# Sliding-window attention feeding a gated MLP on one core: attention tiles of 96 queries replaced by blocks of 32 queries by 64 keys

## The chip, the cores and the metric

The kernel runs on 1 core of one Trainium2 chip. The metric is the device time of one execution in microseconds (us). The kernel before took 1094.05 us (median of 3 runs, 1093.78 to 1095.33). About 0.2% of that, some 2.2 us, is what a measurement can tell from no change.

The engines by the profile's names: PE multiplies matrices (PEld is its loading of the stationary operand, which overlaps), DVE is the vector engine, ACT the scalar engine, POOL the third elementwise engine, SP issues most transfers.

## What is computed

```python
q, k, v: (8, 8, 576, 64)          # batch, heads, positions, head size, float32
rel = pos[:, None] - pos[None, :]
plain   = (rel >= 0) & (rel < 32)                     # heads 0 to 3
dilated = (rel >= 0) & (rel < 128) & (rel % 4 == 0)   # heads 4 to 7
attn = softmax(where(mask, q @ k.T / 8, -1e9)) @ v
x = attn as (4608 tokens, 512)    # 8 heads side by side
g, val = x @ w_gate, x @ w_val    # 512 -> 1536
out = (silu(g) * val) @ w_out     # 1536 -> 512
```

Every query sees at most 32 keys: the 32 last positions, or every fourth of the last 128.

## The kernel before, in words

The 4608 tokens are cut into 12 chunks of 384 (CH). The MLP of a chunk takes 12 steps (NF), one for each 128 of the 1536 hidden features; `s` counts all 144 steps, `ci, f = divmod(s, 12)`. A step issues 36 products of 128x128 by 128x384 in float32r: 12 for the gate into `bank_g` and 12 for the value into `bank_v` (`gv_mm`, L457), and, for the step before, 12 into four output banks (`out_mm`, L493). The factor three comes from a split: x, h and the weights are kept as a high part rounded to float32r and a low part, and high-high, high-low and low-high are added up. Around the products stand `act_tanh` (ACT, L465), `dve_u` and `dve_h` (DVE, L470 and L474), `h_hi` (ACT, L478) and `h_lo` (POOL, L483). `dve_u` empties `bank_g`, so the next step's gate products wait for it.

The weights are loaded during the first chunk, as 24 units of raw 64-bit words, two for each step: a transfer by SP (`w_load`, L198), E on ACT (L207), B on DVE (two operations, L213 and L214), H on ACT (L224) and L on POOL (L228). B of a unit also issues the load of a later unit. The last four units share one buffer, `spare["r"]`.

The attention of chunk c fills `x_hi[c % 2]` and `x_lo[c % 2]` for the chunk's MLP. A chunk has four packs, one for each pair of heads (`ORDER`: the two dilated pairs, then the two plain ones). It is done in three ways:

- Chunk 0, ahead of the MLP, already in blocks of 32 queries by 64 keys (`b_scores` to `b_x_lo`, L532 to L603), from an order written out by hand (L648). A block product has 64 contracting rows and 32 output columns, so that two heads use PE's two halves of rows and four blocks its four quarters of columns. Each float32 product is two instructions in the trace. Twelve blocks make three groups of 128 rows.
- Chunk 1, during chunk 0's MLP, in tiles of 96 queries (64 in the dilated packs that cross a sequence's end), two tiles of a pair of heads at a time: mask and scores into `bank_s` (`scores_pair`, L295 and L298), maximum (L313), four exponentials with sums (L322), division on POOL (L350).
- Chunks 2 to 11, one tile at a time: `split_hi` and `split_lo` (L358 on ACT, L363 and L364 on POOL) cut queries and keys into float32r parts, `scores` multiplies twice with 256 columns (L370), `maxima` adds parts and mask and takes the maximum on DVE (L383 to L385), `exps` runs two exponentials with sums on ACT (L392), `norm` divides on POOL (L400).

In the last two, `transposes` (L408) turns two tiles for both heads (four instructions), `pt_copy` (L413) takes the result to SBUF, and once for a pack `av_mm` (L421) multiplies with v, one head in each half of PE's columns, two instructions a product; `x_copy_hi` (L440) and `x_copy_lo` (L444) write x. Chunk 1 has 18 tiles, chunks 2 to 11 have 166, in 40 packs of 4 or 5.

The order of the work is the program's order, which the scheduler of the language keeps except where data is not there yet. The loops from L690 spread a chunk's tiles over 10 to 12 steps of the chunk before: scores behind the gate products (after `act_tanh`, ahead of `dve_u`) or behind `h_lo`, transposes behind the value products, `av_mm` after `out_mm`.

## Time and profile before

| what | value |
|---|---|
| time, median of 3 runs | 1094.05 us |
| the profiled execution's own time | 1093.62 us |
| its span on the core | 1091.8 us |
| first product of the MLP starts | 30.66 us |
| first product of step 12 (chunk 1) starts | 142.44 us |
| first product of step 132 (chunk 11) starts | 1007.85 us |
| PE busy from 142.44 us on | without a gap, in all but the last microseconds |
| transfers, mean over the span | 78 GB/s |

In a row of a group: line, engine, operation, output <- inputs, size of the stationary operand (rows*columns), size of the moving one (partitions x elements), count, then total busy us, mean ns of one, idle us before them and what ended it. A row of the chain or of a timeline begins with its start and its length in us. Mean ns of a PE instruction is its latency; instructions overlap, so what one costs is the distance between starts.

### The profile page before, as it was taken

To read this page: it belongs to the slowest core of one execution; us is meant where nothing else is said; L and a number is where in the kernel's file an instruction comes from. 1 tells how busy PE (TensorE), PEld (TensorE's weight loads), DVE (VectorE), ACT (ScalarE), POOL (GpSimd) and SP (SyncE) were. 2 spreads that over 40 slices of the span, in tenths; PEclk is the share of its full clock that TensorE was granted. 3 is DMA by queue.
4 is the path that set the end of the run, shared out by engine and by line. 5 is a ranking of instruction groups with operands and counts; after the bars stand their busy time and mean duration, and the time that the engine had idled before them with its cause. 6 is when DMAs were issued, how large, how long until landed. Compare 5 with 4: busy or idle time off the path is not lost.

```text
span 1091.8 us, 19600 instructions
## 1 busy us (share of the span) xinstructions
PE 1058.4 (97%) x7106; PEld 1027.4 (94%) x7106; DVE 509.5 (47%) x1309; ACT 489.5 (45%) x1416; POOL 517.2 (47%) x681
## 2 busy tenths in 40 slices
PE   6887999999999999999999999999999999999997
PEld 4776999999999999999999999999999999999997
DVE  5797445445444444345444454444444444442211
ACT  4565544454445445445444544444444544542111
POOL 1564555555455555454545554454555555541111
PEclk7888999999999999999999999999999999999999
DMA  7763332232122213112213222113122221300000
GB/s 284 246 213 110 125 99 62 62 90 71 47 86 69 69 46 99 53 53 81 66 55 90 61 63 81 52 54 91 53 55 79 75 66 49 98 19 2 29 1 30
DMA packets 62801, 85.48 MB, mean 78 GB/s; under 512 B 5008, under 2 KB 58608, under 8 KB 62704
## 3 DMA queue, kind: packets, MB, share of 16 engines
q1 hardware_dynamic: 62416, 83.64, 25.5%
q8 instruction: 56, 0.92, 0.4%
q10 hardware_dynamic: 288, 0.59, 0.1%
q14 instruction: 41, 0.34, 0.1%
HBM read 74.77 MB, written 9.44 MB: 77 GB/s over the span
## 4 chain that ended last, share of the span: by engine, by line
PE 90%; DVE 5%; ACT 2%; DMA 2%; issue 1%; POOLq 0%; POOL 0%; ACTq 0%; SPq 0%; DVEq 0%
PE bg L457 27%; PE bo L493 26%; PE bv L457 26%; PE bs L370 4%; PE bt L421 3%; PE bt L408 3%; DVE y L214 2%; DVE y L213 1%; DMA words<-w 1%; ACT words L207 1%; DMA qkb<-qkb 1%; ACT e L322 1%; ACT w L224 0%; DVE ma L313 0%; PE fx L561 0%
## 5 line engine op out<-in xcount | busy, mean ns | idle before, releaser
L457 PE MATMUL bg<-xh,w 128*128 128x384 f32 x1152 | 326.1, 344 | 3.4 <-DVE xl L603 3.4
L457 PE MATMUL bv<-xh,w 128*128 128x384 f32 x1152 | 319.8, 338 | 0.0
L493 PE MATMUL bo<-hh,w 128*128 128x384 f32 x1152 | 300.6, 342 | 0.0
L457 PEld LDWEIGHTS bg<-xh,w 128*128 128x128 f32 x1152 | 213.5, 190 | 9.4 <-DVE xl L603 3.8
L483 POOL TENSOR_TENSOR hl<-t,hh 128x384 fp32r<-128x384 f32 x144 | 146.8, 1020 | 152.8 <-PE bo L493 144.3
L363 POOL TENSOR_TENSOR cmb<-raw,cmb 128x256 fp32r<-128x256 f32 x166 | 122.4, 738 | 197.1 <-ACT cmb L358 186.4
L457 PEld LDWEIGHTS bv<-xh,w 128*128 128x128 f32 x1152 | 211.2, 188 | 0.6
L465 ACT ACTIVATE t<-bg 128x384 f32<-128x384 f32 x144 | 70.8, 491 | 308.1 <-PE bg L457 278.3
L493 PEld LDWEIGHTS bo<-hh,w 128*128 128x128 f32 x1152 | 203.1, 188 | 1.0 <-issue 1.0
L493 PE MATMUL bo<-hl,w 128*128 128x384 f32 x576 | 194.5, 338 | 1.5 <-POOL hl L483 1.5
L457 PE MATMUL bg<-xl,w 128*128 128x384 f32 x576 | 195.7, 340 | 0.0
L457 PE MATMUL bv<-xl,w 128*128 128x384 f32 x576 | 194.4, 338 | 0.0
L392 ACT ACTIVATE s<-s,nm 96x128 f32<-96x128 f32 x332 | 130.8, 395 | 113.5 <-DVE nm L385 111.9
L383 DVE SCALAR_TENSOR_TENSOR s<-bs,consts 96x256 f32<-96x256 f32 x166 | 69.6, 419 | 239.7 <-PE bs L370 238.2
L400 POOL TENSOR_TENSOR s<-s,zr 96x256 f32<-96x256 f32 x166 | 101.6, 612 | 134.2 <-DVE zr L399 110.1
L470 DVE SCALAR_TENSOR_TENSOR t<-t,bg 128x384 f32<-128x384 f32 x144 | 78.5, 545 | 84.7 <-ACT t L465 84.5
L493 PEld LDWEIGHTS bo<-hl,w 128*128 128x128 f32 x576 | 108.1, 188 | 2.2 <-POOL hl L483 2.2
L474 DVE SCALAR_TENSOR_TENSOR t<-t,bv 128x384 f32<-128x384 f32 x144 | 79.7, 553 | 64.9 <-PE bv L457 63.9
L457 PEld LDWEIGHTS bg<-xl,w 128*128 128x128 f32 x576 | 109.7, 190 | 0.0
L457 PEld LDWEIGHTS bv<-xl,w 128*128 128x128 f32 x576 | 108.4, 188 | 0.4
L364 POOL TENSOR_TENSOR cmb<-raw,cmb 64x192 fp32r<-64x192 f32 x166 | 98.7, 594 | 13.0
L358 ACT CAST cmb<-raw 128x448 fp32r<-128x448 f32 x166 | 93.1, 561 | 11.5 <-issue 6.9
(67 smaller groups left out, 990.7 us busy)
## 6 DMA issues: line engine op xcount, KB each, us to landing
raw<-qk SPq DMA_DIRECT2D x166, 224.0 KB, 2.5
words<-w SPq DMA_DIRECT2D x24, 768.0 KB, 5.4
v<-v SPq DMA_DIRECT2D x36, 256.0 KB, 3.0
out<-ot SPq DMA_DIRECT2D x48, 192.0 KB, 2.0
v<-v SPq DMA_DIRECT2D x8, 320.0 KB, 3.3
raw<-qk SPq DMA_DIRECT2D x16, 112.0 KB, 2.7
vb<-vb SPq DMA_DIRECT2D x4, 390.0 KB, 6.3
qkb<-qkb SPq DMA_DIRECT2D x2, 400.0 KB, 7.6
```

The lines of the kernel that those rows point to most:

```text
L358: nc.scalar.copy(out=c[:, 0:448], in_=st[g]["raw"])
L363: nc.gpsimd.tensor_tensor(out=c[:, 448:704], in0=r[:, 192:448], in1=c[:, 192:448], op=ALU.subtract)
L364: nc.gpsimd.tensor_tensor(out=c[D:P, 0:192], in0=r[D:P, 0:192], in1=c[D:P, 0:192], op=ALU.subtract)
L383: nc.vector.scalar_tensor_tensor(out=s, in0=ps[:, :, 1, :], scalar=0.125, in1=mk, op0=ALU.mult, op1=ALU.add)
L392: nc.scalar.activation(out=s[:, h, :], in_=s[:, h, :], func=AF.Exp, bias=nm[:, h:h + 1], accum_out=z[:, h:h + 1])
L400: nc.gpsimd.tensor_tensor(out=s, in0=s, in1=z.unsqueeze(2).broadcast_to([TQ, 2, P]), op=ALU.mult)
L457: nc.tensor.matmul(out=bank[:, :CH], lhsT=wt[f][:, o:o + P], rhs=x[:, k, :], start=n == 0, stop=n == 3 * NK - 1)
L465: nc.scalar.activation(out=t, in_=bank_g[:, :CH], func=AF.Tanh, scale=0.5)
L470: nc.vector.scalar_tensor_tensor(out=t, in0=t, scalar=1.0, in1=bank_g[:, :CH], op0=ALU.add, op1=ALU.mult)
L474: nc.vector.scalar_tensor_tensor(out=t, in0=t, scalar=0.5, in1=bank_v[:, :CH], op0=ALU.mult, op1=ALU.mult)
L483: nc.gpsimd.tensor_tensor(out=hl, in0=hst[i][0], in1=hst[i][1], op=ALU.subtract)
L493: nc.tensor.matmul(out=bank_o[j][:, :CH], lhsT=wt[f][:, o:o + P], rhs=x, start=f == 0 and n == 0, stop=f == NF - 1 and n == 2)
```

## The change

All packs of all chunks use the blocks that chunk 0 used. `Pack` lays out a pack: 12 blocks in three groups, or, in the dilated packs that cross a sequence's end, 16 blocks in four groups (48 queries of a residue make a block of 32 and one of 16). Chunks 1 to 11 have 140 groups in 44 packs. The order of pairs becomes (2, 0, 3, 1), so that a pack of four groups stands beside packs of three.

Two PSUM banks, `two`, replace `bank_s` and `bank_t`: head h of a pair writes bank h. Each pack m is visited twice, at places counted in thirds of a step (behind the gate products, behind the value products, behind the output products):

- A: `results(m - 1)`, the products with v; `scores(m)`, the products of queries and keys; the loads of pack m's v and of pack m+1's queries and keys; then on DVE `norm(m - 1)` and `shift(m)`, on ACT `exps(m)`.
- B: `turn_y(m - 1)` into bank 0 and `turn_e(m)` into bank 1, each one transpose of 128x128 a group; `keys(m)` copies the second to SBUF on ACT; `x_copy_hi` and `x_copy_lo` write x.

In steady state A stands behind the gate products and B behind the value products, A four thirds ahead of its B. The scores of chunks 2 to 11 are now plain float32 (no split), with the mask added by DVE; in chunk 1 the mask goes through PE (`masked`). v has a column of ones, so the sum comes out of the product and the division moves behind it, from POOL to DVE. The transposes of dilated packs multiply with a permuted identity, so the copies to x read in order. Gone are the splits of queries and keys, the sums on ACT, and all of the attention's work on POOL.

Ahead of the MLP the order by hand is another: among other moves, the copies of the last pack (H3, L3) come ahead of the third B of the weights, and packs 2 and 3 turn into other banks. The second load of weights comes earlier on SP.

```diff
+class Pack:
+    def __init__(self, c, p):
...
+        for b, lo, n in SEGMENTS[c % 3]:
+            per = n // self.step
+            nb = -(-per // BQ)
...
+        self.groups = [[(b, q, n, BQ * i, nq + k) for i, (b, q, n, k) in enumerate(blocks)][a:a + 4]
+                       for a in range(0, len(blocks), 4)]
...
+    def scores(m, two, masked):
+        t, ng = st[m]["qk"], pk(m).ng
+        a = 512 - BK * ng
+        if masked:
+            for h in range(2):
+                nc.tensor.matmul(out=two[:, h, a:], lhsT=ident16, rhs=masks_of(m), start=True, stop=False,
+                                 skip_group_check=True)
+        for g, blocks in enumerate(pk(m).groups):
+            for j, (_, _, _, q, k) in enumerate(blocks):
+                for h in range(2):
+                    r = slice(D * h, D * h + D)
+                    nc.tensor.matmul(out=two[BQ * j:BQ * j + BQ, h, a + BK * g:a + BK * g + BK],
+                                     lhsT=t[r, q:q + BQ], rhs=t[r, k:k + BK], start=not masked,
+                                     stop=not masked or g == ng - 1, skip_group_check=True)
+
+    def shift(m, two, pool, masked):
...
+        if not masked:
...
+            nc.vector.tensor_tensor(out=ev, in0=s, in1=mk, op=ALU.add)
+            s = ev
+        nc.vector.reduce_max(out=mx, in_=s, axis=mybir.AxisListType.X)
+        nc.vector.tensor_tensor(out=ev, in0=s, in1=mx.unsqueeze(3).broadcast_to([P, 2, ng, BK]), op=ALU.subtract)
+        st[m]["e"] = e
+
+    def exps(m):
+        e = st[m]["e"]
+        nc.scalar.activation(out=e, in_=e, func=AF.Exp, scale=0.125)
...
+    def results(m, two):
+        t, v = st[m]["pt"], st[m]["v"]
+        for i in range(4 * pk(m).ng):
+            g, j = divmod(i, 4)
+            for h in range(2):
+                r = slice(D * h, D * h + D)
+                nc.tensor.matmul(out=two[BQ * j:BQ * j + BQ, h, (D + 1) * g:(D + 1) * (g + 1)],
+                                 lhsT=t[r, BQ * i:BQ * i + BQ], rhs=v[r, i, :], start=True, stop=True,
+                                 skip_group_check=True)
...
-    for what in ("Q0 Q1 S0 X0 T0 S1 K0 X1 A0 M0 T1 N0 K1 U0 A1 H0 L0 N1 Q2 U1 S2 H1 X2 L1 T2 W0 K2 A2 W1 N2 "
-                 "Q3 U2 S3 W2 X3 H2 L2 T3 W3 K3 W0 A3 W1 N3 W2 U3 W3 H3 L3 W0 W1 W2 W0 W1").split():
+    for what in ("Q0 Q1 S0 X0 T0 S1 K0 X1 A0 M0 Q2 T1 N0 K1 W0 U0 S2 A1 H0 X2 N1 Q3 L0 T2 K2 W1 U1 A2 W0 H1 "
+                 "S3 W2 X3 N2 T3 L1 K3 W3 U2 W1 H2 A3 W0 N3 W2 U3 L2 H3 W3 L3 W1 W0 W2 W1").split():
...
+    visit = {}
+    for m in range(4, NPK + 1):
+        c, n = divmod(m - 4, 4)
+        first_a, first_b = ((0, 8, 15, 23), (4, 12, 20, 27)) if c == 0 else ((-6, 3, 12, 21), (-2, 7, 16, 25))
+        visit[36 * c + first_a[n]] = "A", m
+        visit[36 * c + first_b[n]] = "B", m
+
+    def attend(at):
+        what, m = visit.get(at, ("", 0))
+        if what == "A":
+            if m > 4:
+                results(m - 1, two)
+            if m < NPK:
+                scores(m, two, m < 8)
+                load_v(m, apool, nc.sync)
+                if m + 1 < NPK:
+                    load_qk(m + 1, apool, nc.sync)
+            if m > 4:
+                norm(m - 1, two, apool)
+            if m < NPK:
+                shift(m, two, apool, m < 8)
+                exps(m)
+        elif what == "B":
+            if m > 4:
+                turn_y(m - 1, two[:, 0])
+            if m < NPK:
+                turn_e(m, two[:, 1])
+                keys(m, two[:, 1], apool)
+            if m > 4:
+                x_copy_hi(m - 1, two[:, 0])
+                x_copy_lo(m - 1, two[:, 0])
...
         if live:
             gv_mm(ci, f, 0)
             act_tanh(s)
-        if cur:
-            front(cur[0])
+        attend(3 * s)
         if live:
             dve_u(s)
...
             gv_mm(ci, f, 1)
-        for pr in do_pairs[s]:
-            transposes(pr, bank_t)
-            pt_copy(pr, bank_t)
+        attend(3 * s + 1)
         if live:
             dve_h(s)
             h_hi(s)
...
         if s > 0:
             out_mm(s - 1)
...
+        attend(3 * s + 2)
```

617 lines of the change are left out of this document (128 added, 489 removed).

## The prediction

> **What bounds the kernel now.** I read the page first: busy shares and slices, then the chain that ended last.
>
> ```profile
> PE 1058.4 (97%) x7106; PEld 1027.4 (94%) x7106; DVE 509.5 (47%) x1309; ACT 489.5 (45%) x1416; POOL 517.2 (47%) x681
> PE   6887999999999999999999999999999999999997
> PE 90%; DVE 5%; ACT 2%; DMA 2%; issue 1%; POOLq 0%; POOL 0%; ACTq 0%; SPq 0%; DVEq 0%
> PE bg L457 27%; PE bo L493 26%; PE bv L457 26%; PE bs L370 4%; PE bt L421 3%; PE bt L408 3%; DVE y L214 2%; DVE y L213 1%; DMA words<-w 1%; ACT words L207 1%; DMA qkb<-qkb 1%; ACT e L322 1%; ACT w L224 0%; DVE ma L313 0%; PE fx L561 0%
> ```
>
> The reader is to see one bound and one exception. PE is full from the fifth slice on; only the first four, some 110 us, have holes, and the 2% and 1% of DVE's weight conversion (L214, L213) lie there. Attention's own share of the chain is L370, L421 and L408. Busy shares say nothing about what an instruction costs, so I took the chain in order of time in one steady chunk, then the starts of the stages.
>
> ```profile
> 301.89 0.81 PE bt L421 x16
> 302.70 2.31 PE bg L457 x12
> 305.01 0.24 PE bs L370 x2
> 305.25 2.11 PE bv L457 x12
> 307.36 0.33 PE bt L408 x4
> 307.69 2.13 PE bo L493 x12
> ```
>
> Here the chain is PE alone: everything on the other engines is covered, and what attention puts on PE adds straight to the time.
>
> ```profile
> 30.66 4.21 PE bg L457 x12
> 142.44 2.11 PE bg L457 x12
> 1007.85 2.12 PE bg L457 x12
> 1014.16 2.12 PE bg L457 x12
> 1020.49 2.12 PE bg L457 x12
> ```
>
> These are the first gate products of the MLP, of step 12 and of steps 132, 133 and 134. A step without attention takes 1020.49 - 1014.16 = 6.33 us. From 142.44 to 1007.85 there are 120 steps in 865.4 us; 120 x 6.33 = 759.6 are the MLP's, so attention costs 105.8 us there, 2.65 for each of 40 packs. The rows above agree: a pack of four tiles is 4 x 0.24 + 2 x 0.33 + 0.81 + 0.20 (the gate products behind L421 take 2.31 instead of 2.11) = 2.63.
>
> **Steady chunks: what goes and what comes.** What goes from PE is that 105.8 us. What comes is two visits a pack. The blocks run in the trace of before already, for chunk 0:
>
> ```profile
> 9.42 0.73 PE L575 MATMUL fr<-vb,bpt 64*32 64x65 f32 x48
> 10.07 0.55 PE L561 MATMUL fk<-ident_p,be 128*128 128x128 f32 x3
> 10.55 0.54 PE L542 MATMUL fs<-qkb 64*32 64x64 f32 x34
> L575 PE MATMUL fr<-vb,bpt x48: 213/217/241, 9.4 to 9.9; 64*32 64x65 f32 x48
> L542 PE MATMUL fs<-qkb x8: 240/240/240, 10.6 to 10.6; 64*32 64x64 f32 x8
> ```
>
> A pack of three groups has 24 block products, 48 instructions, in each of `results` and `scores`. The 126 groups of 40 packs make 3.15 a pack, 50.4 instructions.
>
> - Spacing of starts: results (0.73 - 0.22) / 47 = 10.9 ns; scores (0.54 - 0.24) / 33 = 9.1 ns. So 50.4 x 10.9 = 0.55 us and 50.4 x 9.1 = 0.46 us.
> - Changes between whole array and blocks: from the last start of the results (9.42 + 0.51 = 9.93) to the next transpose is 0.14. From that transpose to the blocks is 0.48 for three transposes of 128 columns, which at L408's rate (0.33 / 4 x 128 / 96 = 0.11 each) take 0.33, so 0.15 for the change. The gate or value products behind pay 0.20 more, as behind L421. Sum 0.49, once per A.
> - A: 0.55 + 0.46 + 0.49 = 1.50. B: 6.3 transposes x 0.11 + 0.02 = 0.72. A pack: 2.22 us, 40 packs 88.8.
>
> Gain 105.8 - 88.8 = 17.0 us. The number of changes of mode stays one visit a pack (L421 before, A after), so it is no term. The splits on ACT and POOL, the sums and the division cost nothing now, being under PE, and bring nothing.
>
> The bounds come from the same blocks in the cold part:
>
> ```profile
> 19.75 0.98 PE L575 MATMUL fr<-vb,bpt 64*32 64x65 f32 x48 [0.57 <-ACT bpt L566]
> 19.74:20.65 0.91, 0.91 (x48) 0.50 0.19 74
> L575 PE MATMUL fr<-vb,bpt x48: 307/312/313, 19.7 to 20.4; 64*32 64x65 f32 x48
> ```
>
> At a granted clock of 0.50 the spacing is (0.98 - 0.31) / 47 = 14.3 ns. If the steady stage paid that, A grows by 100.8 x 14.3 ns - 1.01 = 0.43, 17 us in 40 packs: gain 0. If blocks went with the clock alone, 7.1 ns, A shrinks by 0.29: gain 29. I take 9.1 and 10.9, since the steady stage runs at full clock.
>
> **What must stay covered.** A puts its vector work ahead of `dve_u` in DVE's queue, and the next gate products wait for `dve_u`.
>
> ```profile
> L585 DVE TENSOR_TENSOR by<-fr,bz 128x384 f32<-128x384 f32 x4 | 2.2, 555 | 0.1
> L550 DVE TENSOR_REDUCE bm<-fs 128x6 f32<-128x384 f32 x4 | 2.2, 554 | 5.7 <-PE fs L542 5.7
> L551 DVE TENSOR_TENSOR be<-fs,bm 128x384 f32<-128x384 f32 x4 | 2.2, 551 | 0.1
> L584 DVE RECIPROCAL bz<-bz 128x6 f32<-128x6 f32 x4 | 0.7, 186 | 0.1
> L583 DVE TENSOR_SCALAR bz<-fr 128x6 f32<-128x6 f32 x4 | 0.6, 160 | 1.4 <-PE fr L575 1.4
> L470 DVE SCALAR_TENSOR_TENSOR t<-t,bg 128x384 f32<-128x384 f32 x144 | 78.5, 545 | 84.7 <-ACT t L465 84.5
> qkb<-qkb SPq DMA_DIRECT2D x2, 400.0 KB, 7.6
> vb<-vb SPq DMA_DIRECT2D x4, 390.0 KB, 6.3
> ```
>
> `norm` is 0.16 + 0.19 + 0.56 = 0.91, `shift` with the mask (a third operation, taken like L551) 3 x 0.55 = 1.65, `dve_u` 0.55: 3.1 us after the blocks end at about 1.3, with some 0.3 between instructions 4.7. The next gate products start at 1.50 + 2 x 2.11 = 5.7. So 1.0 us is to spare; with four groups in `shift`, a third more on it, 0.4 remain. Without that cover each 0.1 us a visit would cost 4 us. ACT's exponential and `h_hi` behind it have the same slack. The loads of a pack (v behind `results`, queries and keys behind `scores`, on SP) are issued nine thirds, some 21 us, ahead of use; transfers of that size landed in 7.6 and 6.3 at the densest moment of the trace. At B, `dve_h` stands behind transposes and three copies: 0.72 and four operations of about 0.55 are 2.9, against 0.72 + 4.22 until the next value products. Nothing becomes late. Step 132 and what follows (84 us) has no attention and stays.
>
> **Ahead of step 12.** This stage is not PE's alone.
>
> ```profile
> 30.66:142.44 111.78, 97.72 (x575) 91.98 (x576) 75.95 (x108) 62.95 (x152) 60.65 (x46) 0.92 0.52 170
> by line: DVE y L214 18.8%; PE bg L457 13.5%; DVE y L213 10.9%; DMA words<-w 7.9%; PE bv L457 7.8%; ACT words L207 6.8%; issue 6.7%; PE bo L493 5.7%; ACT e L322 5.1%; PE bt L421 2.9%; ACT w L224 2.4%; DVE ma L313 2.3%; PE bs L298 1.6%; DVE t
> 27.32 0.48 ACT L599 CAST xh<-fx 128x384 fp32r<-128x384 f32 x1 [0.82 <-PE fx L561]
> 27.70 2.44 DVE L214 SCALAR_TENSOR_TENSOR y<-words,y 128x768 int32<-128x768 int32 x1
> 30.07 0.54 DVE L603 TENSOR_TENSOR xl<-fx,xh 128x384 fp32r<-128x384 f32 x1
> 45.27 1.05 POOL e L350
> ```
>
> PE is busy 97.72 of 111.78 us and waits for weights. On this stage's chain the attention of chunk 1 has ACT e 5.1, L421 2.9, L313 2.3 and L298 1.6%, that is 5.7, 3.2, 2.6 and 1.8 us, and one division on POOL (45.27). The exponentials, 36 with a read of their sum each, become four; that 5.7 goes, and the division's 1.0. The 7.6 us of PE and DVE come back, I count, in full: five A and B at 2.22 and 2.56 us of vector work in each take the place of 18 tiles' products and maxima. Gain 6.7. Bounds: with no idle left and 5 us less work, the stage would be 93, 19 less; with conversions waiting behind vector work of 2.56 in two of the five visits, 5 more than now.
>
> In the prelude the last copy to x ran at 30.07 because a conversion of weights (27.70) stood ahead of it, though its input was ready at 27.80. The new order turns them round: up to 2.3 us earlier, but the conversion put behind is then the late one, on a chain that L214 leads. I count 1.3. Together 8.0.
>
> **Sum.** 1093.6 (the profiled execution's own time, 0.4 below the median of the runs; its span is 1.8 less) - 17.0 - 8.0 = 1068.6 us.
>
> **Rivals.**
>
> 1. Blocks at the cold price in steady state too. For: the only four-pack stretch on record is half cold. Against: the two warm rows. 1068.6 + 17 = 1085.6. Chance 0.12.
> 2. The first chunk becomes PE's alone. For: POOL's division and ACT's four exponentials, which stood between conversions, go. Against: the last four units of weights share one buffer whatever attention does. About 12 more: 1056.6. Chance 0.11.
> 3. The vector work outruns its cover: `shift` is 0.4 us short of slack in some packs, and an operation there could be slower than L551. At 0.5 us in 40 packs: 1088.6. Against: PSUM sources already in the rows. Chance 0.07.
> 4. Slower: instruction supply. A issues 101 multiplications and as many weight loads in a burst that now takes 48.
>
> ```profile
> 11.77 0.23 PE fr L575 x3
> 11.99 1.24 issue
> 13.23 0.63 PE fr L575 x38
> ```
>
> Amid the results of one pack PE stood 1.24 us with nothing to wait for that the profile shows. If each A met one such gap: 40 x 1.24 = 50, 1118 us. It decides from 25.0 / 40 = 0.63 us a visit on. Against: the bursts at 9.42 and 19.75 run through, and transfers were at their densest here. Chance 0.06. The Trainium skill ("Runtime: NRT & Kernel Launch", Instruction fetch mechanics) has instructions refilled in blocks of 256 and fetched ahead, mostly hidden; by that rule the gap stays rare, and no row here shows a fetch.
> 5. Slower: eight blocks overlap no better than two halves. L421's 16 instructions of 96 columns took 0.81, 51 ns each, 34 at 64 columns; 100.8 x 34 ns is 3.4 instead of 1.01: + 96, 1164 us. Against: 48 starts within 0.65 (9.42 to 10.07) allow at most 13.5 ns. Chance 0.02. The Trainium skill ("TensorE: Matmul & The Clock Gate", Wait — 56ns, not 53.3ns?) says that starts of matmuls never come closer than about 25 ns. By it A would take 1.5 us more and the kernel some 1129; the same row speaks against it for blocks.
>
> **How the numbers follow.** The forecast keeps 0.62. The range runs from between the forecast and the cases with both terms better (29 and 16 instead of 17 and 8, so 1048.6) to the cold price: 1051 to 1087; outside lie rivals 3 (half), 4 and 5 and the extreme of 2. Faster by over 0.2% (2.2 us, about what a measurement of this kernel can tell) are the forecast, 1, 2 and most of 3: 0.90. Within 0.2%: 1 and 3 at their upper ends, 0.02. Slower: 4 and 5, 0.08.
>
> **What would show it.** Starts of steps 12 and 132 are 120 steps and about 848 us apart (865 before), with PE unbroken between. A row of about 1.3 us of blocks behind the gate products, 12 products behind it at 2.3, transposes x6 at 0.7. Step 12 starts near 134. Wrong if the visits take over 2.6 us a pack, if "issue" stands amid blocks, or if gate products wait for DVE's L470 successor.

## The result, and the profile after

| | before | after |
|---|---|---|
| median of 4 runs, us | 1094.35 (1093.78 to 1095.33) | 1046.09 (1044.13 to 1046.80) |
| the profiled execution, us; its span | 1093.6; 1091.8 | 1046.64; 1044.8 |
| ahead of the first gate product, us | 30.66 | 32.77 (+2.1) |
| from there to step 12 | 111.78 | 95.53 (-16.3) |
| step 12 to step 132 | 865.41 | 833.27 (-32.1) |
| step 132 to the end | 83.95 | 83.23 (-0.7) |

The time after is 0.9555 of the time before (95% interval 0.9539 to 0.9572). The kernel became faster by 48 us; the forecast had 25 and its range ended 5 us above the measured time. Of the 47.0 us by which the two spans differ, the steady chunks give 32.1 (17.0 were forecast), the first chunk 16.3 (6.7 forecast), and the prelude takes 2.1 more (1.3 less was forecast). One of the four executions of the kernel with POOL products in a row (below) ran at a granted clock of 0.65 and took 1418 us; its figures go by the other three.

First the page of the kernel after: the engines' busy time, PE by slices, and the chain that ended last by lines.

```profile
PE 1018.1 (97%) x10392; PEld 992.1 (95%) x10392; DVE 360.1 (34%) x690; ACT 257.1 (25%) x506; POOL 192.7 (18%) x172
PE   6798999999999999999999999999999999999997
PE 89%; DVE 5%; DMA 3%; ACT 2%; issue 1%; POOL 0%; POOLq 0%; ACTq 0%; DVEq 0%; SPq 0%
```

PE has 3300 instructions more and is busy 40 us less. DVE's work fell by 149 us, ACT's by 232 and POOL's by 325, and in the steady chunks, where PE alone is on the chain, none of that is in the time: the shares of the chain are nearly those of before. The holes in PE's slices are in the first four, as before; the third and fourth are fuller (8 and 7 before, 9 and 8 after).

The same chain in order of time, in a steady chunk (start, us, engine, tile, line, instructions):

```profile
300.93 2.08 PE bg L309 x12
303.02 0.73 PE two L262 x49
...
303.81 0.49 PE two L222 x28
304.30 2.30 PE bv L309 x12
306.60 2.08 PE bo L345 x12
...
312.84 0.44 PE two L280 x4
313.28 0.33 PE two L246 x3
313.61 2.11 PE bo L345 x12
```

This is one A visit and one B visit of packs with three and four groups. The blocks take 304.30 - 303.02 = 1.28 us and the value products behind them 2.30 instead of 2.08; the seven transposes of B take 0.77. These are the rows that the prediction named (1.3, 2.3, 0.7), and PE is unbroken as it said. Results and scores run into each other without a pause. What the prediction does not have is the 2.08 of the groups without blocks ahead of them: it counted twelve MLP products at 2.11.

The first chunk in one row for each kernel, as in the prediction: stretch, its length, busy time of PE, PEld, DVE, ACT and POOL, granted clock, share and rate of the transfers. This is the kernel after.

```profile
32.77:128.30 95.53, 88.96 (x956) 83.69 (x957) 64.50 (x91) 49.63 (x78) 52.20 (x32) 1.00 0.57 205
```

And PE's waits in that stage, before and then after (who waited for whom, us in all, times, the longest):

```profile
PE bt L421 <- ACT pt L413: 11.2, 3, 5.7
PE bg L457 <- DVE xl L603: 3.4, 1, 3.4
```

```profile
PE bg L309 <- DVE t L322: 2.7, 3, 1.2
PE bg L309 <- DVE xl L297: 2.4, 1, 2.4
PE bv L309 <- DVE t L326: 2.0, 1, 2.0
```

PE idles 14.1 us of 111.8 before and 6.6 of 95.5 after. Two long waits for one copy on ACT (4.9 and 5.7 us) and a short one are gone. The granted clock is 0.92 before. The 1.00 after is too high: that trace has no clock record ahead of 37.03 us, and twelve MLP products ahead of it take 334 ns each, against 174 at full clock. Before, the clock stands at 0.50 up to 35.8 us, from 66.5 to 73.4 and from 97.3 to 104.1; the two later stretches begin 3.2 and 2.0 us behind the starts of the two long waits (63.3 and 95.3), and the kernel after has none behind 37.03.

### The profile page after: what moved, and what is told of

It reads as the page before. It is cut to its first block, busy times and chain, and to the rows that moved or that the text cites. A ratio compares the mean times of both kernels' runs of the same rounds, so it can differ in the third digit from the quotient of the medians.

```text
span 1044.8 us, 23074 instructions
## 1 busy us (share of the span) xinstructions
PE 1018.1 (97%) x10392; PEld 992.1 (95%) x10392; DVE 360.1 (34%) x690; ACT 257.1 (25%) x506; POOL 192.7 (18%) x172
## 4 chain that ended last, share of the span: by engine, by line
PE 89%; DVE 5%; DMA 3%; ACT 2%; issue 1%; POOL 0%; POOLq 0%; ACTq 0%; DVEq 0%; SPq 0%
PE bv L309 28%; PE bg L309 27%; PE bo L345 27%; PE two L262 2%; DMA words<-w 2%; PE two L222 2%; DVE y L149 2%; DVE y L148 2%; PE two L280 1%; PE two L246 1%; ACT words L142 1%; DMA qkb<-qkb 1%; ACT w L159 0%; DVE be L237 0%; POOL w L163 0%
## 5 line engine op out<-in xcount | busy, mean ns | idle before, releaser
L309 PE MATMUL bg<-xh,w 128*128 128x384 f32 x1152 | 319.3, 337 | 6.2 <-DVE t L322 2.7
L345 PE MATMUL bo<-hh,w 128*128 128x384 f32 x1152 | 296.5, 338 | 0.0
L322 DVE SCALAR_TENSOR_TENSOR t<-t,bg 128x384 f32<-128x384 f32 x144 | 79.7, 553 | 428.9 <-ACT t L317 428.4
L345 PEld LDWEIGHTS bo<-hh,w 128*128 128x128 f32 x1152 | 205.7, 188 | 0.0
L330 ACT CAST hh<-t 128x384 fp32r<-128x384 f32 x144 | 74.1, 514 | 305.5 <-DVE t L326 305.4
L326 DVE SCALAR_TENSOR_TENSOR t<-t,bv 128x384 f32<-128x384 f32 x144 | 79.6, 553 | 94.7 <-PE bv L309 94.2
L163 POOL TENSOR_TENSOR w<-y,w 128x768 fp32r<-128x768 f32 x24 | 45.4, 1901 | 63.9 <-ACT w L159 63.7
L297 DVE TENSOR_TENSOR xl<-two,xh 128x384 fp32r<-128x384 f32 x44 | 24.5, 557 | 56.4 <-ACT xh L293 56.4
L262 PEld LDWEIGHTS two<-vb,pt 64*32 64x32 f32 x2240 | 25.9, 105 | 11.1 <-issue 11.1
L222 PE MATMUL two<-qkb 64*32 64x64 f32 x2240 | 34.2, 226 | 0.0
L354 DVE COPY ot<-bo 128x384 f32<-128x384 f32 x24 | 13.4, 557 | 60.1 <-POOL hl L335 30.2
```

Source lines behind the costliest of these rows:

```text
L163: nc.gpsimd.tensor_tensor(out=lo, in0=wst.pop(u).bitcast(F32), in1=hi, op=ALU.subtract)
L222: nc.tensor.matmul(out=two[BQ * j:BQ * j + BQ, h, a + BK * g:a + BK * g + BK], lhsT=t[r, q:q + BQ], rhs=t[r, k:k + BK], start=not masked, ...
L262: nc.tensor.matmul(out=two[BQ * j:BQ * j + BQ, h, (D + 1) * g:(D + 1) * (g + 1)], lhsT=t[r, BQ * i:BQ * i + BQ], rhs=v[r, i, :], start=Tru ...
L297: nc.vector.tensor_tensor(out=xl, in0=src, in1=xh, op=ALU.subtract)
L309: nc.tensor.matmul(out=bank[:, :CH], lhsT=wt[f][:, o:o + P], rhs=x[:, k, :], start=n == 0, stop=n == 3 * NK - 1)
L322: nc.vector.scalar_tensor_tensor(out=t, in0=t, scalar=1.0, in1=bank_g[:, :CH], op0=ALU.add, op1=ALU.mult)
```

## The experiments

All medians stand beside runs of the kernel before on the same chip, with the ratio to it. Where a stage is compared, the first chunk runs from the first gate product of step 0 to that of step 12, the steady stage from there to step 132; taken from the products' own starts these are 111.6 and 865.4 us before, 95.4 and 833.3 after.

### Do the MLP's products depend on where their operands lie?

The chain's groups of twelve MLP products come in two lengths, 2.08 and 2.11 to 2.12 us, at full clock in both, and which it is goes by the chunk's parity and by whether the feature is one of the last two. Those are the things that change the operands' places in SBUF: x has two buffers, and the weights of the features 10 and 11 a pool of their own. The change moved the buffers, since other tiles around them went. The bytes at which they start in a partition, modulo 512, as a build of the kernels gives them:

| | w0 to w9 | w10, w11 | x even | x odd | h | t |
|---|---|---|---|---|---|---|
| before | 64 | 480 | 64 | 192 | 192 | 192 |
| after | 0 | 480 | 0 | 0 | 0 | 0 |

Groups whose moving operand starts in line with their weights are short in both kernels; of the other distances some are short and some long. Five kernels test this with unused bytes alone.

**The whole placement undone.**

```diff
...
+    padp.tile([P, 32], F32, name="pad0")          # ahead of the h pool
...
+    xpool.tile([P, 96], F32, name="pad1")         # behind the odd x tiles
...
+    lastw.tile([P, 16], F32, name="padw")         # behind w10, w11
```

> The changed kernel, with unused bytes that put every tile of the MLP (x of the odd chunks, t, h, the last weights) where it stands in the kernel before against the weights, modulo 512; the scratch tiles of attention stay. Theory (of the change's 48 us some 6 are this placement and no part of attention): the steps 12 to 132 take 6 us more, 839 to 840, as before's MLP products did, and the time is 1051 to 1053 us. Rival (the MLP's products became faster for what runs beside them): no change, 833 us between the steps and 1046 in all.

Measured: 1052.40 us median (1051.72 to 1053.73), ratio 0.962 (0.9605 to 0.9634), and 838.8 us between the steps 12 and 132, 5.5 more than after. Its chain in chunk 11, where no attention runs, shows the long groups back:

```profile
976.91 2.11 PE bo L348 x12
979.02 2.12 PE bg L312 x12
981.13 2.11 PE bv L312 x12
```

against this of the changed kernel in the same chunk:

```profile
967.85 2.08 PE bg L309 x12
969.93 2.08 PE bv L309 x12
972.01 2.08 PE bo L345 x12
```

So some 6 of the change's 48 us have nothing to do with attention's work: they are a by-product of where the tiles came to lie.

**Only the odd chunks' x moved.**

```diff
+    xpool.tile([P, 32], F32, name="pad0")
     x_hi.append(xpool.tile([P, NK, CH], F32R, name="xh1"))
     x_lo.append(xpool.tile([P, NK, CH], F32R, name="xl1"))
+    xpool.tile([P, 32], F32, name="pad1")
```

> The changed kernel, with 128 unused bytes per partition ahead of the odd chunks' x tiles and 128 behind, so that these alone lie 128 bytes off; the weights and the other tiles stay. Theory (place): gate and value groups of the odd chunks' features 0 to 9, 2.08 us in the changed kernel, go to 2.11 (120 groups at +0.033 us: about +4 us, some 1050 us), and those of the even chunks stay. Rival (company, by what runs beside the products): no change, 1046 us.

Measured: 1049.25 us (1048.36 to 1050.00), ratio 0.9578 (0.9565 to 0.9591), 2.9 us more between the steps 12 and 132. Gate and value groups of the odd chunks' features 0 to 9 are at 2.11 to 2.12, those of the even chunks at 2.08. The groups of the features 10 and 11 in odd chunks went the other way, from 2.12 to 2.08, which lowers the sum below the 4 us expected: there x came out of the costly distance.

```profile
1023.20 2.11 PE bv L309 x12
...
1027.39 2.08 PE bg L309 x12
```

These rows lie on the border in chunk 11: value of feature 9, then the gate of feature 10. Over all these kernels, the distance from the weights' start to the moving tile's, modulo 512, is 0, 160 or 224 in the short groups and 32, 96 or 128 in the long ones.

**The last weights put in line.**

```diff
                 wt.extend(lastw.tile([P, 2 * WB], F32R, name=f"w{f}") for f in range(NF - LATE, NF))
+                lastw.tile([P, 120], F32, name="padw")
```

> The changed kernel, with an unused tile of 480 bytes per partition among the tiles of the last weights, so that w10 and w11 start at the same place modulo 512 as w0 to w9. Theory (place): the 72 groups of the features 10 and 11, at 2.12 us, go to 2.08: about 2.9 us less, some 1043.2 us. Rival (late weights are slow for a reason of their own, such as the place in the address range or when they were written): no change, 1046 us.

Measured: 1044.34 us (1043.97 to 1044.70), ratio 0.9533 (0.9520 to 0.9546); 1.8 us less between the steps 12 and 132. The intervals of this ratio and of the changed kernel's overlap, so the time alone would not decide it; the rows do. The gate of feature 10 in chunk 11, which is at 2.12 after (1024.01), is here at 2.08:

```profile
1021.82 2.08 PE bg L310 x12
```

**The kernel before, put in line: a miss.**

```diff
...
+    padp.tile([P, 96], F32, name="padh")          # ahead of the h pool
...
+                lastw.tile([P, 104], F32, name="padw")
```

> The kernel before, with 384 unused bytes per partition ahead of the first pool and 416 behind the words of the last units, so that the six tiles of weights w0 to w9, w10 and w11, the x tiles and the h tiles all start at 64 modulo 512; nothing else is changed. Theory (place): a group of 12 MLP products takes 2.08 us or 2.11 to 2.12 us by where the moving operand lies against the weights, and 264 of before's 432 groups are of the slow kind. All go to 2.08: about 264 x 0.033 = 8.7 us less, some 1085.5 us, with no group left at 2.11 or 2.12. Rival (company): the 0.03 us is lost to what the other engines do beside the products (64-row blocks leave them less to do, and so the change removed it): no change, 1094 us, with the slow groups where they were.

Measured: 1094.01 us (1092.25 to 1095.57), ratio 0.9989 (0.9980 to 0.9998). Gate and out groups went to 2.08 as the theory has it. But the value groups went from 2.08 and 2.11 to 2.13 in both parities, which took back all that was won. In a step of a steady chunk, and in chunk 11, where no attention runs beside them:

```profile
523.70 2.13 PE bv L460 x12
...
1018.19 2.08 PE bv L460 x12
```

The same products, from the same tiles, are long only beside attention, and not by their first product alone: the starts within such a group are 171 to 185 ns apart, mostly 173 to 174 in chunk 11. So it looks as if a second placement counts: that of attention's tiles and of t, which the 384 bytes had moved as well.

**The same with those left in their places.**

```diff
         t = hpool.tile([P, CH], F32, tag="t", name=f"t{i}")
+        if i == 0:
+            hpool.tile([P, 96], F32, tag="padh", bufs=1, name="padh")
...
     x_lo.append(xpool.tile([P, NK, CH], F32R, name="xl1"))
+    xpool.tile([P, 32], F32, name="pad1")
...
+                lastw.tile([P, 104], F32, name="padw")
```

> The kernel before, with w10, w11, the odd chunks' x tiles and the h tiles at 64 modulo 512 as w0 to w9 are, but the t tiles and the scratch tiles of attention left at 192 and 448, where they are in the kernel before (the earlier kernel had moved them to 64 and 320 as well; its gate and out groups went to 2.08 us as expected, but the value groups of both parities to 2.13, and the sum stayed). Theory (two placements count: moving operand against weights, and the tiles that the other engines stream meanwhile against both): all groups at 2.08, some 8.7 us less, 1086 us. Rival (value groups are slow for the place of the x tile alone): value groups at 2.13 again, within 2 us of 1094.

Measured: 1088.81 us (1087.60 to 1090.37), ratio 0.9952 (0.9939 to 0.9965). All MLP groups that stand behind other MLP groups are at 2.08 to 2.09, and the value groups behind the scores' products too:

```profile
521.15 2.09 PE bv L458 x12
```

The kernel before becomes 5.6 us faster by some 930 unused bytes; 8.7 were expected. The Trainium skill ("SBUF — State Buffer", SBUF: two separate sides) says that PE never waits for another engine's access to SBUF. The value groups of these two kernels, 2.13 and 2.09 by the place of others' tiles, speak against it, by 2%. The weights and the tiles of x and h lie alike in the two kernels. Which tile of which engine it is was not tried.

### What do blocks and changes of mode cost?

**The results' products twice.**

```diff
-        for i in range(4 * pk(m).ng):
+        for i in list(range(4 * pk(m).ng)) * (2 if m >= 8 else 1):
```

> The changed kernel, with the products of the results issued a second time, right behind the first, for the 40 packs of the chunks 2 to 11 (the second writes what the first wrote). It prices a block product behind another one in place. By the groups of the changed kernel's trace, where 49 or so instructions of the results take 0.73 us and 28 of the scores 0.49, an instruction costs 10 to 15 ns: 40 packs x about 50 products make +20 to +29 us, 1066 to 1075 us, and the cover of the vector work stands aside (no wait of PE). Rival (blocks run at the spacing of 25 ns that the prediction's fifth case had): +50 us, 1096 us. Rival (what counts is mode changes and not products, second pass nearly free): under +10 us.

Measured: 1071.81 us (1068.90 to 1072.07), ratio 0.9775 (0.9760 to 0.9790), 24.8 us more between the steps 12 and 132. It holds a find: six times PE stands with nothing to wait for that the profile shows, 0.2 to 0.86 us, 3.7 us in all. Three times it is amid the blocks, as here, and three times in the value products behind a visit (288.7, 546.8, 804.7).

```profile
308.37 1.35 PE two L262 x87
309.73 0.26 PE two L222 x16
309.99 0.86 issue
310.85 0.45 PE two L222 x29
```

The rest is 21.1 us for 2016 instructions, 10.5 ns each: the prediction's 10.9, and no trace of 25. A long visit alone does not bring them, since the other 34 have none. Counted in the trace's PE and PEld instructions, the sequencer's included, they stand behind number 6849, 7361, 13249, 13761, 19649 and 20161, all 193 beyond a multiple of 256. The gap at 11.99 that the prediction's fourth rival started from stands behind number 449, again 193 beyond one, and 256 is the block that this rival speaks of. So its gaps exist and fit the supply of instructions, though no record shows a fetch. Here each comes in or right behind a burst of some 150 block instructions and as many weight loads; with the 100 of the changed kernel there is none of over 0.1 us in the steady stage.

**The A visit in two.**

```diff
+        if m > 8:
+            visit[36 * c + first_a[n] - 2] = "R", m
...
+        if what == "R":
+            results(m - 1, two)
+            norm(m - 1, two, apool)
...
```

> The changed kernel, with the results' products and the norm of the packs 8 to 47 in a visit of their own, two thirds ahead of the A visit that held them (behind value products). The same products, one more change between whole array and blocks and back for each of 40 packs. It prices that change, the term of the sum that the prediction put at 0.49 us. By the prediction's figure: +19.6 us, 1066 us. By the idle of 0.25 us on the weight loads ahead of line 262 and 0.08 to 0.20 more on the group behind: 0.33 to 0.45 each, +13 to +18 us. If a change costs only the drain of the product ahead: under 0.15 each, under +6 us.

Measured: 1061.44 us (1060.07 to 1062.10), ratio 0.970 (0.9687 to 0.9714), 15.3 us more between the steps 12 and 132: 0.39 for each of 39 changes (the last pack's results had a visit to themselves already).

```profile
322.33 0.66 PE two L262 x45
322.99 2.28 PE bo L345 x12
...
327.36 0.79 PE two L222 x53
328.14 2.28 PE bv L309 x12
```

Half of it is in sight here: each group of products behind blocks takes 2.28 instead of 2.08. An A visit is then 50.4 x 10.5 ns = 0.53, and the prediction's 0.46 for the scores, and 0.39: 1.38. The chain's rows of the steady stage give (24.77 + 21.82) / 40 for L262 and L222 and 0.20 behind, 1.36.

### Where did the first chunk's 16.3 us come from?

By the starts of the products, each counted up to the next start and not beyond its own end, the first chunk divides as follows (us):

| | length | MLP products | attention's | PE idle |
|---|---|---|---|---|
| before | 111.6 | 83.0 | 14.5 | 14.1 |
| after | 95.4 | 78.1 | 10.7 | 6.6 |
| before, divisions on DVE | 107.0 | 81.8 | 14.6 | 10.7 |
| before, results later | 110.6 | 84.1 | 14.4 | 12.1 |
| before, both | 105.2 | 81.5 | 14.4 | 9.3 |
| after, idle POOL products | 95.2 | 78.7 | 10.5 | 6.0 |
| after, POOL products in a row | 95.9 | 79.8 | 10.3 | 5.7 |
| after, idle ACT exponentials | 98.0 | 80.3 | 10.9 | 6.7 |
| after, unit 19 early | 97.4 | 81.1 | 10.4 | 5.9 |
| after, B late | 98.7 | 79.5 | 11.2 | 8.0 |
| after, order of before | 95.7 | 78.7 | 10.5 | 6.5 |

So attention's own products are 3.8 us of the 16.3, waits 7.5, and the same MLP products took 4.9 less. Of these 4.9, some 3.3 are products at half clock: 32 of them took 10.8 us before, against 5.6 at 174 ns each, and twelve took 4.0 after, against 2.1. The other 1.6 were spent at full clock and are not explained. In the kernels of this table every stretch at 0.50 that begins in the first chunk begins 2 to 4 us behind the start of a wait of PE of 1.7 us or more, and each wait of 3.1 us or more in it had one; so waits seem to cost clock on top of themselves. Kernels with the same first chunk as after came out between 94.6 and 96.1, which is how far these lengths can be trusted.

**Idle work on POOL, and on ACT.**

```diff
...
                 keys(m, two[:, 1], apool)
+                if m < 8:
+                    for _ in range(3):
+                        ev = st[m]["e"].rearrange("q g h k -> q (g h k)")[:, :384]
+                        nc.gpsimd.tensor_tensor(out=scr[:, :384], in0=ev, in1=ev, op=ALU.mult)
```

> The changed kernel, with three idle GpSimd products of 128x384 behind each B visit of the packs 4 to 7 (12 in all, about 1.07 us each by the row of hl, 12.9 us: what the kernel before had there in its rows of e and cmb). They read the exponentials and write a scratch tile that nobody reads. In question: why the first chunk became 16.3 us shorter, where 6.7 were forecast. Theory (VectorE's unpacking stalls while GpSimd works): the row of y at L149, 23.6 us in the changed kernel and 34.0 before for the same 20 instructions, grows by 5 us or more, and step 12 starts 5 to 10 us later than at 128.1. Rival (ScalarE's queue): L149 stays within 2 us and so does step 12. Rival (fewer hand-overs between engines per pack): step 12 stays within 2 us, too.

Measured: 1048.27 us (1046.42 to 1049.79), ratio 0.9574 (0.9558 to 0.9590); first chunk 95.2, line 149 26.7 us for 22 instructions where it was 26.5. No effect is clear of the scatter. In the second kernel six exponentials on ACT (`nc.scalar.activation(out=scr[:, :384], in_=ev, func=AF.Exp, scale=-1.0)`) stand in the same place.

> The changed kernel, with six idle exponentials of 128x384 on ScalarE behind each B visit of the packs 4 to 7 (24 in all, about 0.48 us each, 11.5 us: nearly what the kernel before had more on ScalarE in the first chunk, 62.95 against 49.63 us). Theory of GpSimd: step 12 stays within 2 us of 128.1. Rival (ScalarE's queue): it starts 5 to 10 us later. Rival (fewer hand-overs): within 2 us.

Measured: 1048.83 us (1047.79 to 1049.03), ratio 0.9573 (0.9558 to 0.9587); first chunk 98.0, with 0.1 us more idle and the products slower at a granted clock of 0.95. That is hardly more than the scatter, and not the 5 to 10 us of the theory. Load on either engine as such, in the place where it was put here (behind the copy of the keys), is not the cause.

**Weights.**

```diff
-        pool = spare["r"] if late(u) or ("r" in spare and u % 4 == 3) else rpool
+        pool = spare["r"] if late(u) or ("r" in spare and u % 4 == 3 and u < 19) else rpool
```

> The changed kernel, with the words of unit 19 in the pool of the early units and not in the spare tile, so that the load of unit 20 needn't wait for unit 19's unpacking. Theory (after the change the first chunk ends with the weights: four loads of 4.1 to 4.5 us, one after the other by the single spare tile, stand on its chain): one turn of 7.5 to 8.3 us less on that chain; TensorE's own 89 us from 32.8 set the next bound at 121.7, so step 12 starts 4 to 6.4 us earlier, and the time is some 1040 to 1042 us. Rival (TensorE's own work is the bound): no change within 1 us.

Measured: 1047.15 us (1045.38 to 1048.89), ratio 0.9559 (0.9541 to 0.9577); first chunk 97.4. My theory fell: the serial loads stand on the chain of the kernel after, but one turn less of them brings nothing. PE has 89 us of its own work there and idles only 6.

**The copy's reader put later, in the kernel before.** The results' products of chunk 1 go behind the next step's gate products:

```diff
...
+        for i in held:
+            turn_in(i)          # av_mm and the copies to x, as before
         if cur:
             front(cur[0])
...
```

> The kernel before, with the results' products of chunk 1 (line 421) put behind the next step's gate products, one group of MLP products later than they stood; nothing else is moved. In question: where the first chunk's 16.3 us come from. By the starts and ends of TensorE's instructions they are 7.5 us of waits (11.2 us of them before, in three waits of line 421 for ScalarE's copy at line 413), 5.1 us of MLP products at a lower granted clock, and 3.8 us of attention's own products. Theory (distance: the copy stands in ScalarE's queue behind a weight step that waits for VectorE, and before had only one group, 2.1 us, between the copy and its reader; the changed kernel has three or four): the waits at line 421 fall from 11.2 us to under 6, and step 12 starts 4 to 10 us earlier than at 142.3, so 1084 to 1090 us. Rival (the engines are simply less loaded after the change): the wait moves to the new place, step 12 within 2 us.

Measured: 1093.05 us (1092.08 to 1093.96), ratio 0.9988 (0.9979 to 0.9998). The waits at L421 fell from 11.2 to 3.7 as expected, yet the first chunk is only 1.0 us shorter: waits of the transposes for the copy to x, in the same PSUM bank, and smaller ones came in their place, and the MLP's products took 1.1 us more.

```profile
PE bt L421 <- ACT pt L413: 3.7, 2, 2.8
...
PE bt L408 <- DVE xl L444: 3.3, 2, 2.3
```

**The reader put close, in the kernel after.** `first_b` of chunk 1, (4, 12, 20, 27), becomes (7, 14, 22, 29), two or three thirds later.

> The changed kernel, with the B visits of the packs 4 to 7 put three thirds later, one third ahead of the next pack's A visit, so that between the copy of the keys and the results' products stands one group of products (2.1 us), as before the change. Theory (distance): waits of TensorE at line 262 for ScalarE's copy at line 252 come back, 4 to 10 us in the first chunk, and its MLP products take some us more at a lower clock; step 12 starts 4 to 12 us later than at 128.1. Rival (less load): no wait of more than 1 us there, step 12 within 2 us.

Measured: 1053.44 us (1048.94 to 1054.34), ratio 0.9632 (0.9616 to 0.9647). The profiled execution is the fastest of the four, with a first chunk of 98.7; in it PE waits 8.0 us at L262, but for the copy to x, whose bank the results overwrite, and not for the keys:

```profile
PE two L262 <- DVE xl L297: 8.0, 3, 4.2
```

So the wider spacing of the visits is worth several us, by another hand-over than I had thought.

**POOL's rows.** The timeline of before, around one of its long steps of weight unpacking (start, duration, engine, line, operation; in brackets the idle before it and who ended that):

```profile
89.35 1.25 POOL L350 TENSOR_TENSOR e<-e,zr 96x256 f32<-96x256 f32 x1 [3.46 <-DVE zr L349]
90.56 1.74 POOL L228 TENSOR_TENSOR w<-y,w 128x768 fp32r<-128x768 f32 x1
91.02 4.75 DVE L214 SCALAR_TENSOR_TENSOR y<-words,y 128x768 int32<-128x768 int32 x1
92.26 0.99 POOL L483 TENSOR_TENSOR hl<-t,hh 128x384 fp32r<-128x384 f32 x1
93.20 1.75 POOL L228 TENSOR_TENSOR w<-y,w 128x768 fp32r<-128x768 f32 x1
95.81 0.83 ACT L224 CAST w<-y 128x768 fp32r<-128x768 f32 x1 [4.81 <-DVE y L214]
...
100.99 1.55 PE L421 MATMUL bt<-pt,v 128*64 128x64 f32 x20 [5.66 <-ACT pt L413]
```

L214 takes 0.96 us alone. Here it takes 4.75 and ends 0.8 behind a row of POOL instructions that ran without a gap to 94.95. The row had piled up behind a division that waited 3.46 us for DVE. ACT's next weight step waits 4.81 for L214, and the copy that PE needs (L413, at 100.62) is queued on ACT further behind; PE idles 5.66, the longer of the two long waits. At 79.45 stands another such step, of 3.73. The Trainium skill ("SBUF — State Buffer", SBUF: two separate sides) has DVE and POOL share a pair of ports under an exclusive lock, held for a whole instruction. The trace agrees that DVE stands still meanwhile, 4.75 us for a step of 0.96; it adds that DVE did not get in between the instructions of the row. The change took the division away. In the kernel before, one word does the same:

```diff
-        nc.gpsimd.tensor_tensor(out=e[:, :n], in0=e[:, :n], in1=z.unsqueeze(2).broadcast_to([TQ, n, P]),
+        nc.vector.tensor_tensor(out=e[:, :n], in0=e[:, :n], in1=z.unsqueeze(2).broadcast_to([TQ, n, P]),
...
```

> The kernel before, with the ten divisions of chunk 1 (line 350) on VectorE instead of GpSimd; nothing else is moved. In question, still: why the first chunk became 16.3 us shorter, of which 7.5 are waits of TensorE and 5.1 the lower clock behind them. In the trace of before VectorE's unpacking step (line 214, 0.96 us when alone) takes 3.73 and 4.75 us at 79.45 and 91.02, and ends 0.8 us after a row of three GpSimd instructions that ran without a gap (78.67 to 82.37, 90.56 to 94.95); the row had piled up behind a division that waited for VectorE. Theory (rows of GpSimd hold VectorE up; the change took the division away): the row of line 214 falls from 34.0 to under 28 us, TensorE's waits for ScalarE's copy at line 413 from 11.2 to under 6, and step 12 starts 4 to 12 us earlier than at 142.3, though VectorE has some 6 us more to do. Rival (VectorE's own load is what binds): step 12 later by up to 6 us. Rival (neither): within 2 us.

Measured: 1089.60 us (1089.41 to 1090.21), ratio 0.9954 (0.9940 to 0.9967); first chunk 4.6 us shorter although DVE has ten operations more. L214 in before, in this kernel, and its successor L149 after (busy time, mean ns of one):

```profile
L214 DVE SCALAR_TENSOR_TENSOR y<-words,y 128x768 int32<-128x768 int32 x21 | 36.4, 1735 | 0.4
```

```profile
L214 DVE SCALAR_TENSOR_TENSOR y<-words,y 128x768 int32<-128x768 int32 x21 | 29.9, 1422 | 0.4
```

```profile
L149 DVE SCALAR_TENSOR_TENSOR y<-words,y 128x768 int32<-128x768 int32 x22 | 26.5, 1203 | 0.4
```

The waits at L421 fell less than expected, to 9.6, and the long one shows why. The step of L214 ahead of it is short now, and PE waits nearly as long:

```profile
89.87 1.52 DVE L214 SCALAR_TENSOR_TENSOR y<-words,y 128x768 int32<-128x768 int32 x1
...
96.61 1.55 PE L421 MATMUL bt<-pt,v 128*64 128x64 f32 x20 [4.99 <-ACT pt L413]
```

In both kernels the copy starts 4.8 us behind ACT's weight step (95.81 and 100.62 before, 91.42 and 96.24 here). Between them in ACT's queue stand `act_tanh` and the next pair's four exponentials (L322), which wait for DVE's maximum; they stand ahead of the copy at the first long wait too. So the row of POOL made the weights late, but it accounts for little of PE's long wait. Of the 4.6 us, 1.6 are less wait at L421, 2.0 two waits of PE for POOL itself (L350 and L483, 1.0 each) that are gone, and 1.2 the MLP's products; the start of the scores waits 0.2 longer. The changed kernel has one exponential for a pack in place of four for each pair of tiles. What that alone is worth no run shows.

The reverse, rows put into the kernel after, failed:

```diff
...
             h_hi(s)
+            if 0 < s < 11:
+                nc.gpsimd.tensor_tensor(out=scr[:, :CH], in0=hst[s][0],
+                                        in1=ones[:, 0:1].broadcast_to([P, CH]), op=ALU.mult)
             h_lo(s)
```

> The changed kernel, with one idle GpSimd product of 128x384 (about 1.1 us) in each of the steps 1 to 10, between the copy h_hi and the subtraction h_lo: it waits for VectorE's h as before's division waited for VectorE's sums, and runs in one row with the subtraction and the weights' step behind it. The earlier idle products stood elsewhere and did not hold VectorE up: line 149 took 25.8 us for 21 instructions, against 25.5. Theory (rows of GpSimd): line 149 grows from 25.5 us by 4 or more, and step 12 starts 3 to 10 us later than at 128.1. Rival (GpSimd has nothing to do with it): line 149 within 2 us, step 12 within 2 us.

Measured: 1047.27 us (1046.52 to 1048.49), ratio 0.9567 (0.9553 to 0.9582); first chunk 95.9, L149 26.4 us for 21 where it was 25.5. A row harms, it seems, only where an unpacking step starts in it and PE's next operand comes soon behind; that the wider spacing of the kernel after is what protects it is argued, not shown.

**Both edits in the kernel before.**

> The kernel before, with both edits: chunk 1's divisions on VectorE (alone: 5.1 us less, VectorE's line 214 from 36.4 to 29.9 us for 21 instructions, waits at line 421 from 11.2 to 9.6) and chunk 1's results' products one group later (alone: waits at line 421 from 11.2 to 3.7, and 1.4 us less). Theory (two causes, each of which hides the other: rows of GpSimd make the weight step late, and the copy stands in ScalarE's queue behind it, close to its reader): together more than the sum, step 12 at 131 to 135, 1082 to 1087 us. Rival (they add up): 1088 us. Rival (the wait only moves): 1089 to 1091 us, step 12 at 137 or later.

Measured: 1087.90 us (1086.88 to 1088.30), ratio 0.9940 (0.9923 to 0.9956); first chunk 105.2. They add up, no more. Of the 16.3 us, then, 3.8 are attention's own products, and 6.4 can be had in the kernel before by moving the division off POOL and the reader away from the copy. The 6 that are left (waits 2.7, MLP products 3.4) no edit here brought or took away. Their cause stays open: the number of hand-overs (ten pairs of tiles before, four packs after) and the exponentials ahead of the copy are two candidates.

### The prelude, and the best version

The prediction had the last copy to x earlier, since the new order puts it ahead of a conversion of weights. In the trace after, it is behind two more of them than in the order by hand (L149 at 27.81 and 30.35):

```profile
30.35 1.89 DVE L149 SCALAR_TENSOR_TENSOR y<-words,y 128x768 int32<-128x768 int32 x1
30.45 0.48 ACT L293 CAST xh<-fs 128x384 fp32r<-128x384 f32 x1 [0.82 <-PE fs L280]
32.17 0.54 DVE L297 TENSOR_TENSOR xl<-fs,xh 128x384 fp32r<-128x384 f32 x1
```

Line 297's step stands ahead of both in the order written by hand, but not in DVE's queue, and its input came at 30.93, while the second L149 ran from 30.35 to 32.24. So the old order was put back, as the string of `for what in` alone.

> The changed kernel, with the order of the first chunk's attention as the kernel before has it (the same steps of the same packs; only their order differs). The prediction had the first MLP product 1.3 us earlier than before's 30.66; it came 2.1 later, at 32.77. Theory (the new order does it: weight steps stand ahead of the last pack's on VectorE): the first product at 30 to 31.5, and step 12 moves by less than that, since the weights end the first chunk: 0 to 1.5 us less in all, if the weights don't start later. Rival (the longer hand-overs of the joint PSUM banks do it): first product at 32.5 or later, in either order.

Measured: 1043.74 us (1041.70 to 1045.04), ratio 0.9526 (0.9510 to 0.9542). The first gate product starts at 30.10 instead of 32.77, and step 12 at 125.8 instead of 128.1: most of the gain is carried through, more than expected, which fits a first chunk that PE and not the weights bounds. With the last weights in line as well:

> The changed kernel, with the last weights at the same place modulo 512 as the others, and the first chunk's attention in the order that the kernel before has: the two edits that gained by themselves (1.2 to 1.8 and 2.4 us). If they add up: some 1041.5 to 1042.5 us. If both only moved the first stage by chance: 1044 to 1046.

Measured: 1041.62 us (1039.93 to 1043.12), ratio 0.9517 (0.9504 to 0.9530), the best of all kernels here, 4.5 us below the changed kernel. The two gains add up.

## Why the prediction was wrong, point by point

The spans differ by 47.0 us and 25.0 were forecast. Of the 22.0 that are missing, the steady chunks hold 15.1, the first chunk 9.6 and the end 0.7; the prelude went 3.4 the other way.

- **The bound, right.** PE alone sets the steady stage, before and after; the work taken off ACT, POOL and DVE brought nothing there. Rivals 1, 3, 4 and 5 did not come: products at 10.5 ns, PE busy in all of the 833 us, no gap in a visit of 100 block instructions. For the fifth the prediction named the Trainium skill ("TensorE: Matmul & The Clock Gate", Wait — 56ns, not 53.3ns?), by which starts come no closer than some 25 ns: here block products on separate parts of the array start 10.5 ns apart. The fourth rival's gaps are real, as the doubled results show, but the changed kernel has none in the steady stage.
- **"120 x 6.33 = 759.6 are the MLP's", the step that failed in the steady stage.** The 6.33 us is a step of chunk 11 in before, all of whose groups are long ones. On the chain of before, the MLP's groups in the 120 steps come to 757.8 us, without what the groups behind L421 pay more; attention was 107.6 and not 105.8. And the step did not stay what it was: after, the groups come to 751.9. That the other terms of a step stay was taken for granted. It made 5.9 us of gain that no working on attention could show, and the runs with unused bytes show it to be the placement.
- **A at 1.50, B at 0.72: the terms that were mis-sized.** Measured 1.36 and 0.68, (13.75 + 13.42) / 40 for L280 and L246. The products were right (0.53 and 0.46); the change of mode is 0.39 and not 0.49. Attention after takes 81.4 us instead of 88.8. The sum: 17.0 + 1.8 (before dearer) + 7.4 (after cheaper) + 5.9 (placement) = 32.1, the measured gain.
- **The cover, right in the outcome and not in the reason.** It was argued that A's vector work stands ahead of `dve_u` and fits. In the trace `dve_u` (L322) comes first in 33 of the 40 visits, and `dve_h` (L326) among or behind A's work; in the other seven two operations of 0.16 and 0.19 us stand ahead of it. PE waits for none of it in the steady stage:

```profile
324.66 0.55 DVE L322 SCALAR_TENSOR_TENSOR t<-t,bg 128x384 f32<-128x384 f32 x1 [4.19 <-ACT t L317]
325.36 0.16 DVE L271 TENSOR_SCALAR bz<-two 128x6 f32<-128x6 f32 x1
...
326.97 0.69 DVE L236 TENSOR_REDUCE bm<-be 128x8 f32<-128x512 f32 x1
327.64 0.55 DVE L326 SCALAR_TENSOR_TENSOR t<-t,bv 128x384 f32<-128x384 f32 x1
```

- **"Gain 6.7" for the first chunk, the other step that failed.** It read the gain off the chain's shares (the exponentials' 5.7, the division's 1.0). That chain is one path among several that are nearly as long. The stage came near to its own bound instead, "with no idle left and 5 us less work, 93": 95.5. Rival 2, PE alone there, with a chance of 0.11, came nearest: it had 18.7 for the stage; its time of 1056.6 lacks the steady terms. Its reason, that the division and the exponentials between conversions go, is borne out in part only: the division's move is among the 6.4 us, the exponentials were not tried alone. Two things were not read that stood in the trace: L214's steps of up to 4.75 us where it needs 0.96, and the two stretches at half clock behind PE's long waits.
- **The prelude, wrong in sign.** -1.3 was forecast, +2.1 measured; the order in the code was taken for the order in DVE's queue.

## What to carry to other kernels

Take a stage's terms from that stage: a step measured in another chunk carried another placement, and cost 8 us of forecast. Where a stage has holes, its gain is bounded by the idle and the work of its fullest engine that can go, and not by one chain's shares; look there for instructions that take several times their usual time, and see what ran beside them. And before a change is credited with a gain, compare the work that it did not touch.

## What was not expected of the hardware

- Twelve products of 128x128 by 128x384 take 2.08 or 2.11 to 2.12 us by the distance of the moving operand from the weights in SBUF, modulo 512: 2.08 at 0, 160 and 224, more at 32, 96 and 128. It was worth 5.6 us in the kernel before, where 264 of 432 groups were long.
- The same products took 2.13 us beside attention's work and 2.08 without it; with the tiles of that work 128 bytes elsewhere they took 2.09 beside it.
- PE's pauses without a releaser, 0.2 to 1.24 us, stand behind the same count of its instructions modulo 256 (193), in the prelude of before and six times beside visits of some 150 block instructions; beside visits of 100 there was none.
